# Decode attention over two KV caches: K groups and V groups put into two nested TensorE loops, and the loads put into the same order

## The chip, the cores and the metric

One core of a Trainium2 chip. The metric is the device time of one execution in microseconds (us), lower is better. The kernel before took 262.8 us in the median of its first three runs (261.95 to 264.19). "Span" below is the time from the first to the last instruction in a trace; the measured time is about 1.8 us longer than the span in the runs that were profiled. PE is TensorE, DVE is VectorE, ACT is ScalarE, SP is SyncE, which issues the loads here.

## The reference

Two independent decode attentions, A and B, with one query token, 32 query heads, 16 KV heads, head size 128 and a cache of 8192 rows. A uses only the last 2048 rows. The outputs are laid side by side.

```python
def attention(x, k_cache, v_cache, wq, wo, W):      # A: W = 2048, B: W = 8192
    q = (x @ wq).reshape(1, 1, 32, 128).transpose(0, 2, 1, 3)
    k = jnp.repeat(k_cache[:, :, 8192 - W:, :], 2, axis=1)
    v = jnp.repeat(v_cache[:, :, 8192 - W:, :], 2, axis=1)
    p = softmax(jnp.einsum("bhqd,bhkd->bhqk", q, k) * 128 ** -0.5)
    o = jnp.einsum("bhqk,bhkd->bhqd", p, v)
    return o.transpose(0, 2, 1, 3).reshape(1, 1, 4096) @ wo       # x: (1, 1, 576), all bf16
```

Every byte of K, V, wq and wo is used once: 102.8 MB are read, in both kernels.

## The kernel before

K and V are loaded in groups of four slots of 2.1 MB each: group 0 is A, groups 1 to 4 are B. There are four slot buffers for K and four for V. PE transposes K (two halves, "units", per slot), ACT and DVE evict the transposes, PE forms the scores. After K groups 0, 2 and 4 a softmax follows; its result is transposed on PE in the next odd round. PE's work stands in one loop over seven rounds; V of a group is worked on two rounds after its K (LAG = 2). What a round doesn't have is jumped over.

```python
    K_ON = lambda g: g < 5
    V_ON = lambda g: g >= LAG
    ...
    ORDER = ["k0", "k1", "k2", "v0", "v1", "k3", "v2", "v3"]
    for g in range(5 + LAG):
        for what in ORDER:                       # the order in which SP asks for the loads
            s = int(what[1])
            if what[0] == "k" and g < 5:
                load_kv(ks, g, s, kslots, "k", ...)
            if what[0] == "v" and g >= LAG:
                load_kv(vs, g - LAG, s, vslots, "v")
        ...                                      # [cut: wo loads]
        k_on, v_on = g < 5, g >= LAG
        if k_on:
            ...                                  # [cut: q_stage]
            k_transpose(g, 0, 0)
            k_transpose(g, 1, 1)
        if g % 2 == 1:
            softmax_transpose(g, 2)
            scores_zero((g, 2.5, ODD))
        if k_on:
            for u in range(2, 6):
                k_scores(g, u - 2, 2 * u)
                k_transpose(g, u, 2 * u + 1)
            k_scores(g, 4, 12)
        if v_on:
            v_slot(g - LAG, 0, 13)               # 2 x 64 matmuls between two K steps
            v_slot(g - LAG, 1, 14)
        if k_on:
            k_transpose(g, 6, 15)
            k_scores(g, 5, 16)
            k_transpose(g, 7, 17)
            k_scores(g, 6, 18)
        if v_on:
            v_slot(g - LAG, 2, 19)
        if k_on:
            k_scores(g, 7, 20)
            if g in (0, 2, 4):
                softmax_exp(CHUNK[g])
        if v_on:
            v_slot(g - LAG, 3, 21)
            v_keep(g - LAG)
```

The last argument of a step is its place in the loop body. PE's loop is written out from these places: one body, cut into blocks by condition.

```python
            with eng.Fori(0, rounds) as i:
                ...                              # [cut]
                while places:
                    cond = body[places[0]].loop[2]
                    ...                          # n: as many places as share the condition
                    with eng.If(cond(i)):
                        some(places[:n])
                    places = places[n:]
```

A load is issued by SP in program order, and waits there until its slot's last reader is done; so a load that has to wait also holds those behind it (in the trace, A's V loads, whose slots' last reader starts at 28.7 us, go out at 83.61 us, right behind a row of K loads that ends at 83.57 us).

## Time and profile before

| | kernel before |
|---|---|
| time, median (4 runs in all) | 263.5 us |
| span of the profiled run | 259.5 us |
| bytes read | 102.76 MB |
| share of the span that PE / ACT / DVE are busy | 66% / 34% / 31% |
| load rate from 10 to 55 us, and from 90 to 240 us | 427 and 429 GB/s |
| load rate from 55 to 90 us | 292 GB/s (mean of the seven windows below) |

First the page: busy shares, then 40 slices of 6.5 us with the granted clock of PE in tenths, the busy tenths of the DMA engines and the rate. The last line is the DMA queue of kind "instruction", with its packets and MB.

```profile
span 259.5 us, 7521 instructions
PE 172.1 (66%) x3406; PEld 134.3 (52%) x3406; DVE 80.9 (31%) x152; ACT 87.5 (34%) x92; POOL 12.9 (5%) x49
...
PEclk9996589957799999995998586899599555555577
DMA  7999999995478999999999999999999999999992
GB/s 280 394 450 414 434 429 414 442 419 182 200 283 330 422 427 428 437 424 429 432 422 437 424 427 432 422 437 427 424 434 419 437 427 424 434 420 433 429 400 87
...
q8 instruction: 8, 0.13, 0.2%
```

The DMA engines are at nine tenths in all slices but the first, the last and slices 9 to 12 (counted from 0): the loads bound this kernel, and the slices from about 58 to 84 us are a hole in them. The table of windows shows the hole (columns: stretch in us, its length, busy us of the five engines with counts of instructions, clock, DMA share, GB/s):

```profile
55.00:60.00 5.00, 3.90 (x35) 2.95 (x36) 1.38 (x2) 1.02 (x1) 0.24 (x1) 0.50 0.80 341
60.00:65.00 5.00, 3.46 (x45) 2.00 (x43) 3.18 (x4) 1.02 (x1) 0.24 (x1) 0.82 0.64 210
65.00:70.00 5.00, 2.61 (x36) 2.46 (x34) 1.51 (x4) 4.84 (x5) 0.00 (x0) 0.86 0.55 229
70.00:75.00 5.00, 5.00 (x71) 4.24 (x70) 3.17 (x7) 1.76 (x3) 0.00 (x0) 0.80 0.45 141
75.00:80.00 5.00, 5.00 (x86) 3.91 (x84) 2.85 (x5) 3.96 (x5) 0.24 (x1) 1.00 0.87 333
80.00:85.00 5.00, 5.00 (x85) 3.90 (x83) 2.85 (x5) 3.96 (x5) 0.24 (x1) 1.00 0.95 387
85.00:90.00 5.00, 4.25 (x68) 2.64 (x66) 2.37 (x4) 3.03 (x4) 0.47 (x2) 1.00 0.98 403
```

Against 428 GB/s these seven windows lack 4.8 MB, which is 11.1 us of loading.

SP's timeline (start, duration, what, how many; a merged row includes the waits between its issues) shows when it asked for K group 1's last slot, for three slots of K group 2, and for A's first V slots:

```profile
60.92 0.53 SPq L368 DMA_DIRECT2D kslots<-in_B_k_cache_dram  x1
...
71.60 11.97 SPq L368 DMA_DIRECT2D kslots<-in_B_k_cache_dram  x3
83.61 1.25 SPq L368 DMA_DIRECT2D vslots<-in_A_v_cache_dram  x2
```

And PE's timeline in the first round (in brackets: idle time before the row and what ended it; PEq is PE's own sequencer, and "issue" means that PE waited for nothing that the profile shows):

```profile
47.76 0.63 PE L469 MATMUL sacc<-kt,qst 128*32 128x512 bf16 x8
50.78 2.79 PE L449 MATMUL ktps<-ident,kslots 128*128 128x128 bf16 x31 [2.39 <-PEq L208]
56.10 0.29 PE L449 MATMUL ktps<-ident,kslots 128*128 128x128 bf16 x1 [2.52 <-issue]
56.32 1.04 PE L469 MATMUL sacc<-kt,qst 128*32 128x512 bf16 x8
57.29 3.59 PE L449 MATMUL ktps<-ident,kslots 128*128 128x128 bf16 x32
60.82 1.58 PE L469 MATMUL sacc<-kt,qst 128*32 128x512 bf16 x16
63.93 1.95 PE L449 MATMUL ktps<-ident,kslots 128*128 128x128 bf16 x32 [1.54 <-PEq L208]
```

K group 1's last slot goes out at 60.92 us because the last 32 transposes of group 0 are read until then (57.29 + 3.59). PE works at half clock (0.50 granted from 55 to 60 us; 3.59 us for 32 transposes that take 1.96 us elsewhere).

### The profile page before, as it was taken

What the parts mean: (1) busy time and instruction counts of PE and PEld (TensorE: products, weight loads), DVE (VectorE), ACT (ScalarE), POOL (GpSimd) and SP (SyncE); (2) the same over time, 40 slices, a digit from 0 to 9 for tenths busy, and PEclk for the clock granted to TensorE, in tenths of its full rate; (3) what the DMA queues carried; (4) which work ended last, traced back from release to release, by engine and by line L of the source; (5) the groups of instructions that cost most, each with busy time, mean ns of one, the idle gap of its engine ahead of it and who ended that gap; (6) DMA issues with size and microseconds to landing.
All of it is one profiled execution on the core that took longest, in us unless ns stands there. A gap on an engine that the chain in (4) does not pass through costs nothing. (4 is left out here: it accounts for less than half of the span.)

```text
span 259.5 us, 7521 instructions
## 1 busy us (share of the span) xinstructions
PE 172.1 (66%) x3406; PEld 134.3 (52%) x3406; DVE 80.9 (31%) x152; ACT 87.5 (34%) x92; POOL 12.9 (5%) x49
## 2 busy tenths in 40 slices
PE   0264899667699899954995684994574235335665
PEld 0131296445677687834884563883553234224565
DVE  0010245325365465333751122551144002004220
ACT  2000067423857688541671331771332000000000
POOL 7510000000000000000000000000000000000000
PEclk9996589957799999995998586899599555555577
DMA  7999999995478999999999999999999999999992
GB/s 280 394 450 414 434 429 414 442 419 182 200 283 330 422 427 428 437 424 429 432 422 437 424 427 432 422 437 427 424 434 419 437 427 424 434 420 433 429 400 87
DMA packets 8235, 102.92 MB, mean 397 GB/s; under 512 B 1184, under 2 KB 1312, under 8 KB 2080
## 3 DMA queue, kind: packets, MB, share of 16 engines
q1 hardware_dynamic: 7936, 102.77, 94.3%
q8 instruction: 8, 0.13, 0.2%
q10 hardware_dynamic: 288, 0.00, 0.1%
q14 instruction: 3, 0.02, 0.0%
HBM read 102.76 MB, written 0.00 MB: 396 GB/s over the span
## 5 line engine op out<-in xcount | busy, mean ns | idle before, releaser
L449 PE MATMUL ktps<-ident,kslots 128*128 128x128 bf16 x1280 | 89.8, 236 | 23.6 <-PEq L208 21.0
L449 PEld LDWEIGHTS ktps<-ident,kslots 128*128 128x128 bf16 x1280 | 83.2, 107 | 39.7 <-issue 39.7
L455 ACT ACTIVATE kt<-ktps 128x1024 bf16<-128x1024 bf16 x80 | 78.1, 1022 | 71.0 <-PE ktps L449 71.0
L458 DVE COPY kt<-ktps 128x1024 bf16<-128x1024 bf16 x80 | 55.3, 691 | 84.7 <-PE ktps L449 84.7
L540 PE MATMUL opsum<-vslots,ptm 128*32 128x128 bf16 x1280 | 28.4, 257 | 32.8 <-PEq L208 32.8
L540 PEld LDWEIGHTS opsum<-vslots,ptm 128*32 128x32 bf16 x1280 | 24.9, 116 | 38.5 <-issue 37.0
L469 PE MATMUL sacc<-kt,qst 128*32 128x512 bf16 x320 | 27.0, 411 | 0.9 <-issue 0.5
L403 PE MATMUL opsum<-vslots,xpad 128*32 128x512 bf16 x64 | 8.4, 508 | 16.8 <-DVE xpad L388 11.3
L549 DVE TENSOR_TENSOR diag<-opsum,rows 128x512 f32<-128x512 f32 x5 | 3.5, 691 | 43.1 <-PE opsum L540 43.1
L579 ACT ACTIVATE stat<-stat 128x1 f32<-128x1 f32 (+1 forms) x2 | 0.6, 295 | 45.9 <-DVE stat L577 45.9
L403 PEld LDWEIGHTS opsum<-vslots,xpad 128*32 128x32 bf16 x64 | 2.2, 117 | 20.0 <-issue 12.8
L435 POOL COPY qst<-qtm 128x64 bf16<-128x64 bf16 x20 | 4.6, 237 | 139.4 <-PE sacc L469 131.5
L409 ACT ACTIVATE qrow<-opsum 128x512 bf16<-128x512 f32 x2 | 1.2, 597 | 25.8 <-PE misc L403 25.8
L506 ACT ACTIVATE psb<-sacc,stat 128x2048 bf16<-128x2048 f32 x3 | 5.9, 1968 | 10.0 <-DVE stat L500 10.0
L469 PEld LDWEIGHTS sacc<-kt,qst 128*32 128x32 bf16 x320 | 5.3, 95 | 6.9 <-issue 3.0
L403 PE MATMUL misc<-vslots,xpad 128*32 128x512 bf16 x64 | 8.5, 512 | 0.0
L411 DVE CAST qrow<-misc 128x512 bf16<-128x512 f32 x2 | 1.4, 692 | 17.4 <-PE misc L403 17.4
L626 PE MATMUL ktps<-kslots,opj 128*32 128x144 bf16 x184 | 5.3, 305 | 0.8 <-DVE opj L614 0.8
L626 PEld LDWEIGHTS ktps<-kslots,opj 128*32 128x32 bf16 x184 | 4.9, 137 | 1.0 <-issue 1.0
L610 PE MATMUL misc<-acc,pick 128*128 128x32 f32 x16 | 3.0, 343 | 2.5 <-DVE acc L604 1.8
L498 DVE TENSOR_REDUCE stat<-sacc 128x1 f32<-128x1024 f32 x3 | 3.7, 1225 | 2.9 <-PE sacc L469 2.9
L610 PEld LDWEIGHTS misc<-acc,pick 128*128 128x128 f32 x16 | 2.8, 260 | 2.8 <-DVE acc L604 2.0
(66 smaller groups left out, 56.7 us busy)
## 6 DMA issues: line engine op xcount, KB each, us to landing
kslots<-in_B_k_cache_dram SPq DMA_DIRECT2D x16, 2048.0 KB, 22.3
vslots<-in_B_v_cache_dram SPq DMA_DIRECT2D x16, 2048.0 KB, 26.7
kslots<-in_A_k_cache_dram SPq DMA_DIRECT2D x4, 2048.0 KB, 30.0
vslots<-in_A_v_cache_dram SPq DMA_DIRECT2D x4, 2048.0 KB, 19.4
vslots<-in_A_wq_dram SPq DMA_DIRECT2D x2, 2048.0 KB, 9.8
vslots<-in_B_wq_dram SPq DMA_DIRECT2D x2, 2048.0 KB, 20.1
kslots<-in_A_wo_dram SPq DMA_DIRECT2D x2, 2016.0 KB, 23.6
kslots<-in_B_wo_dram SPq DMA_DIRECT2D x1, 2016.0 KB, 31.1
```

The source lines that it names most:

```text
L403: ins = pe.matmul(qps[c][32 * j:32 * j + 32, :], lhsT=xpad[:, P, x, :], rhs=src[:, o:o + 512], start=(u == 0), stop=(u == WQ_UNITS - 1))
L435: add("pool", lambda pool: pool.tensor_copy(qst[:, s * 64:(s + 1) * 64], qtm[:, o:o + 64]), reads=[("qtm", KIND[g])], writes=[("qst", s)], ...
L449: ins = pe.matmul(ktps_bf[q][:, t * 128:(t + 1) * 128], lhsT=kslots[:, s, o:o + 128], rhs=ident[:, :], start=True, stop=True, is_transpose ...
L455: add("act", lambda act, q=q, dst=dst: act.activation(dst, ktps_bf[q], ACT.Copy), reads=[("bank", q)], writes=[("kt", u % NKT, q)], tag="e ...
L458: add("dve", lambda dve, q=q, dst=dst: dve.tensor_copy(dst, ktps_bf[q]), reads=[("bank", q)], writes=[("kt", u % NKT, q)], tag="e%d%d" % ( ...
L469: ins = pe.matmul(sacc[32 * j:32 * j + 32, 512 * half:512 * half + 512], lhsT=qst[:, s * 64 + e * 32:s * 64 + e * 32 + 32], rhs=rhs, start ...
L498: add("dve", lambda dve: dve.tensor_reduce(st(P, C_M + k), sacc[:, :], AX.X, ALU.max), reads=B_S, writes=[("st", P, C_M + k)], tag="max")
L506: return act.activation(psb[:, :].rearrange("p (x g) -> p x g", g=2), src, ACT.Exp, bias=st(P, C_NB + k), scale=SCALE, accum_out=st(P, C_L ...
L540: ins = pe.matmul(opsum[32 * j:32 * j + 32, s * DH:(s + 1) * DH], lhsT=ptm[:, o:o + 32], rhs=vslots[:, s, b * 128:(b + 1) * 128], start=(u ...
L549: return dve.tensor_tensor(diag[:, g % 2, :, :], opsum[:, :].rearrange("p (s d) -> p d s", s=NS), m, ALU.mult)
L610: ins = pe.matmul(misc[:, 0:32], lhsT=pick[:, r, :], rhs=acc[:, d, 32 * r:32 * r + 32], start=(r == 0), stop=(r == 3))
L626: ins = pe.matmul(ktps[P][32 * j:32 * j + 32, 0:OUTW], lhsT=opj[:, P, jj:jj + 32], rhs=view[:, o:o + OUTW], start=(jj == 0), stop=(jj == H ...
```

## The change

The intent is to have V of A loaded while PE works on K group 1, and to have the program of PE and the order of loads agree: PE gets an outer loop over V groups, with an inner loop over the K groups that go before each (0 and 1, then V of A; 2 and 3, then V of group 1; 4, then V of group 2; and the last two V groups). So the code of all K steps now lies in one piece, with the code of the V steps behind it.

```diff
-            places = sorted(body)
-            with eng.Fori(0, rounds) as i:
-                ... [cut: one body, cut into blocks by condition]
+            inner = sorted(p for p in body if body[p].loop[2] is not None)
+            with eng.Fori(0, self.outer) as v:
+                with eng.Fori(*self.rounds_of(v)) as g:
+                    while inner:
+                        ... [cut: blocks by condition, as before]
+                some(sorted(p for p in body if body[p].loop[2] is None))
...
+    V_OF = {1: 0, 3: 1, 4: 2, 5: 3, 6: 4}          # V group worked on at the end of round g
...
-    ORDER = ["k0", "k1", "k2", "v0", "v1", "k3", "v2", "v3"]
-    for g in range(5 + LAG):
-        for what in ORDER:
-            ... [cut]
+    for g in range(7):
+        if g < 5:
+            for s in range(NS):
+                load_kv(ks, g, s, kslots, "k", ...)
+        if g in V_OF:
+            for s in range(NS):
+                load_kv(vs, V_OF[g], s, vslots, "v")
...
-            for u in range(2, 6):
+            for u in range(2, 8):
                 k_scores(g, u - 2, 2 * u)
                 k_transpose(g, u, 2 * u + 1)
-            k_scores(g, 4, 12)
-        if v_on:
-            v_slot(g - LAG, 0, 13)
-            v_slot(g - LAG, 1, 14)
-        ... [cut: the rest of the K steps, with v_slot 2 and 3 between]
+            k_scores(g, 6, 16)
+            k_scores(g, 7, 17)
+            if g in (0, 2, 4):
+                softmax_exp(CHUNK[g])
+        if g in V_OF:
+            for s in range(NS):
+                v_slot(V_OF[g], s, 20 + s, g)
+            v_keep(V_OF[g])
```

The semaphore waits are derived from the order of the program; their small adaptation is cut. Matmuls, evictions and bytes are the same.

## The prediction

> **What bounds the kernel now.** The loads. The 40-slice page has the DMA engines at 9 tenths in all slices but the first, the last and slices 9 to 12; the table of windows gives 424 to 434 GB/s from 10 to 55 and from 90 to 240 us. 102.9 MB at 428 GB/s is 240 of the 259.5 us span. PE (66%), ACT (34%) and DVE (31%) have slack overall. The chain that ended last begins at 233 us (last V slot's matmuls): a 24 us tail of small steps, beside which wo loads until 254 us.
>
> **The hole.** In 5 us windows from 55 to 90 us the rates are 341, 210, 229, 141, 333, 387, 403 GB/s: 10.2 MB where 428 GB/s would move 15.0, so 11.1 us are lost. By SP's timeline and waits, each K slot of groups 1 and 2 is issued only when PE has transposed its old content (60.9, 71.6, about 77, 83 us), and A's V loads, whose slots are free since about 29 us, stand behind group 2's third slot and go out at 83.6 us. The rate is 0 at 61 and at 69 to 72 us. PE is held up there by A's mask, maximum and exp (DVE 1.23 + 1.22, ACT 1.97 us) and by half clock. [...] 0.50 from 53 to 61 us, 32 transposes in 3.59 instead of 1.96 us.
>
> **The change.** Same bytes, matmuls and evictions. A's V loads move directly behind K group 1's last slot (out at 61 to 64 us), A's V matmuls (4 x 1.07 us) behind K group 1. Other V loads keep their rounds, but stand behind four K loads instead of between them. PE gets nested loops: a few more branches (gaps at present ones 0.4 to 1.5 us) on an engine with slack.
>
> **Estimate.** Of the 11.1 us, 3.6 are lost from 56 to 64 us, before anything changes: they stay. From 62 us one K and four V slots queue 10.5 MB, 24.5 us, to 87 us; by then K group 2's first three slots are issued, so the 7.5 us after 64 close. Later, at 2.46 us per half slot of K on PE: V of A at 89 to 94, group 2 to 114; group 3's slots are issued at about 98, 103, 108, 113 us while the queue reaches to 106 and beyond; at 113 us, when B's first V is issued, about 8 us of queue are left. After that PE waits for loads as before, and the tail is unchanged but 7.5 us earlier. Span about 252, time 262.8 - 7.7 = 255.1 us, range 252.5 to 258.5. Faster by over 2% (under 257.5): 0.86; within 2%: 0.13; slower: 0.01.
>
> **What would show it.** A's V issued at 61 to 64 us; over 400 GB/s from 64 to 90 us and on; a dip only at 57 to 64 us; last V matmuls near 225.5 us; the same 24 us tail.
>
> **What would make it wrong.** (1) A new hole at 105 to 125 us, where K groups 2 and 3 follow each other: half clock there (3.6 + 1.0 us per half slot) would eat the 8 us. (2) Loop entry and exit costing several us each. (3) K slot 3 landing late because V shares the queue. (4) A longer tail where the last matmuls meet the wo loads.

## The result, and the profile after

The changed kernel is correct and took 252.34 us in the median of four runs (251.49 to 252.97), against 263.5 us for the kernel before in its four: ratio 0.958, 95% interval 0.9516 to 0.9644. A ratio here is the mean time of one kernel's fast runs over that of the other's in the same rounds, so not quite the ratio of the medians quoted. The time lies just below the range of the prediction (252.5 to 258.5).

On another chip, in 6 runs, the changed kernel took 251.62 us against 260.89 us for the kernel before, ratio 0.9641. The changed kernel is very steady (251.15 to 252.97 over both sets); the kernel before isn't (258.16 to 264.65 over all the sets).

The page after (span 251.2 us): the busy tenths of the DMA engines and the rate in 40 slices of 6.3 us:

```profile
DMA  7999999999999999999999999999999999999980
GB/s 274 396 432 422 432 425 428 417 436 428 428 427 423 428 420 436 421 431 428 431 423 431 431 431 423 431 431 428 425 428 436 423 433 425 433 418 425 423 332 3
```

The hole is gone in full. From the third slice to the 38th none is below 417 GB/s. The first two windows of the former hole:

```profile
55.00:60.00 5.00, 1.30 (x25) 1.16 (x23) 2.63 (x5) 3.46 (x4) 0.00 (x0) 1.00 0.99 423
60.00:65.00 5.00, 5.00 (x89) 4.23 (x87) 3.40 (x7) 3.15 (x4) 0.00 (x0) 1.00 1.03 439
```

SP asks for K group 1's last slot with the third (a merged row, its second issue ends at 52.78 us), and for A's V from 52.83 us on, 8 us sooner than the prediction had it:

```profile
47.14 5.64 SPq L373 DMA_DIRECT2D kslots<-in_B_k_cache_dram  x2
52.83 2.55 SPq L373 DMA_DIRECT2D vslots<-in_A_v_cache_dram  x4
```

And PE, in the same first round, has neither gap nor half clock (1.00 granted from 45 to 55 us):

```profile
47.61 1.96 PE L459 MATMUL ktps<-ident,kslots 128*128 128x128 bf16 x32
49.50 0.82 PE L479 MATMUL sacc<-kt,qst 128*32 128x512 bf16 x8
50.26 1.96 PE L459 MATMUL ktps<-ident,kslots 128*128 128x128 bf16 x32
52.15 0.63 PE L479 MATMUL sacc<-kt,qst 128*32 128x512 bf16 x8
53.15 0.63 PE L479 MATMUL sacc<-kt,qst 128*32 128x512 bf16 x8 [0.37 <-PEq L213]
```

Group 0's scores end at 53.8 us instead of 62.4 us. This is before the moved loads could have done anything: the two kernels issue the same loads in the same order up to K group 1's last slot.

From the last V slot on, the tail has become a little longer. The chain of waits (start, duration, what), before:

```profile
233.20 2.13 PE opsum L540 x64
...
253.50 3.55 PE ktps L626 x112
```

and after:

```profile
223.25 1.92 PE opsum L550 x49
...
244.68 4.06 PE ktps L636 x96
```

The last V slot's matmuls start 9.95 us earlier, and 1.65 us of that are given back by the end of the span (from there to the end: 26.3 us before, 27.95 us after), mostly in the wo matmuls (`ktps`; the last row and one that is cut: 3.50 and 3.55 us before, 4.05 and 4.06 us after) and in small fp32 matmuls; the granted clock of this stretch was 0.62 before and 0.54 after. The rest of the measured 11.1 us is difference between runs: the run of the kernel before that was profiled took 261.28 us, less than its four timed runs (261.95 us or more), and that of the changed kernel was its slowest (252.97 us).

### The profile page after: what moved, and what is told of

It reads as the page before. It is cut to its first block, busy times and chain, and to the rows that moved or that the text cites. A ratio compares the mean times of both kernels' runs of the same rounds, so it can differ in the third digit from the quotient of the medians.

```text
span 251.2 us, 7501 instructions
## 1 busy us (share of the span) xinstructions
PE 167.9 (67%) x3406; PEld 130.6 (52%) x3406; DVE 80.6 (32%) x152; ACT 86.7 (35%) x92; POOL 12.9 (5%) x49
## 3 DMA queue, kind: packets, MB, share of 16 engines
q1 hardware_dynamic: 7936, 102.77, 96.7%
## 5 line engine op out<-in xcount | busy, mean ns | idle before, releaser
L459 PEld LDWEIGHTS ktps<-ident,kslots 128*128 128x128 bf16 x1280 | 76.3, 101 | 28.8 <-issue 28.8
L459 PE MATMUL ktps<-ident,kslots 128*128 128x128 bf16 x1280 | 82.4, 226 | 12.8 <-PEq L213 12.8
L550 PE MATMUL opsum<-vslots,ptm 128*32 128x128 bf16 x1280 | 29.9, 268 | 39.7 <-PEq L213 39.3
L550 PEld LDWEIGHTS opsum<-vslots,ptm 128*32 128x32 bf16 x1280 | 26.3, 121 | 44.2 <-issue 44.1
L479 PE MATMUL sacc<-kt,qst 128*32 128x512 bf16 x320 | 25.9, 392 | 2.0 <-PEq L213 1.8
L636 PE MATMUL ktps<-kslots,opj 128*32 128x144 bf16 x184 | 5.9, 326 | 0.7 <-DVE opj L624 0.7
L620 PE MATMUL misc<-acc,pick 128*128 128x32 f32 x16 | 3.8, 404 | 2.5 <-DVE acc L614 1.8
L620 PEld LDWEIGHTS misc<-acc,pick 128*128 128x128 f32 x16 | 3.6, 328 | 2.9 <-DVE acc L614 2.1
```

Source lines behind the costliest of these rows:

```text
L459: ins = pe.matmul(ktps_bf[q][:, t * 128:(t + 1) * 128], lhsT=kslots[:, s, o:o + 128], rhs=ident[:, :], start=True, stop=True, is_transpose ...
L479: ins = pe.matmul(sacc[32 * j:32 * j + 32, 512 * half:512 * half + 512], lhsT=qst[:, s * 64 + e * 32:s * 64 + e * 32 + 32], rhs=rhs, start ...
L550: ins = pe.matmul(opsum[32 * j:32 * j + 32, s * DH:(s + 1) * DH], lhsT=ptm[:, o:o + 32], rhs=vslots[:, s, b * 128:(b + 1) * 128], start=(u ...
L620: ins = pe.matmul(misc[:, 0:32], lhsT=pick[:, r, :], rhs=acc[:, d, 32 * r:32 * r + 32], start=(r == 0), stop=(r == 3))
L636: ins = pe.matmul(ktps[P][32 * j:32 * j + 32, 0:OUTW], lhsT=opj[:, P, jj:jj + 32], rhs=view[:, o:o + OUTW], start=(jj == 0), stop=(jj == H ...
```

## The experiments

Two theories. **FETCH**: in the kernel before, PE's first pass through the loop body jumps over V code and runs into code of its own that isn't there yet; this holds it from 48 to 56 us, leaves the array at half clock, delays K group 1's last slot from about 52.5 to 60.9 us, and so makes part of the hole. **ORDER**: the load order alone closed the hole, and what changed before 61 us is chance, or a load that landed sooner (called LANDING where it is tested alone).

Reading for FETCH: the page has a DMA queue of kind "instruction" (q8) that moves 8 packets, 0.13 MB, so about 16 KB each, and from 45 to 72 us there are four of them before and one after. That these are blocks of PE's program, and that PE waits for one after a jump, was the assumption when the theory was written; what speaks for it is in sections 3, 4 and 6. Those of the kernel before begin at 47.9, 53.7, 60.7 and 66.7 us, and PE's transposes of the first round and the next resume at 50.78, 56.10, 63.93 and 68.28 us (the last of these waits for A's softmax too, as it does in the changed kernel). These are the lines of that queue for 45 to 72 us, before, then after:

```profile
q8 instruction: 4, 0.07, 1.0%
```

```profile
q8 instruction: 1, 0.02, 0.3%
```

Over the whole execution the changed kernel's page has the same 8 packets: the change doesn't save packets, it moves them. Three of them now begin at 77.8, 84.0 and 90.2 us, where PE comes to the V code and then to the next K group. PE's pauses there (4.07 us before 86.34 us, 2.68 us before 91.09 us) end with landings, of A's last V slot at about 86.2 us and of K group 2's first slot at about 91.0 us. So PE waits for loads there anyway, and the queue of loads stays full (423 GB/s or more in each window from 75 to 95 us).

All experiments gave correct results. The kernels of one call shared a chip and the runs of the kernel before: its medians were 261.51, 260.79 and 260.89 us in the three calls.

| kernel | time, median (range), us | ratio to before, 95% interval |
|---|---|---|
| loads alone | 254.3 (251.88 to 256.97) | 0.9729 (0.965 to 0.9807) |
| two loops, old loads | 269.68 (265.54 to 270.46) | 1.0255 (1.0124 to 1.0386) |
| the same with 128 skipped matmuls | 277.0 (275.16 to 280.38) | 1.0594 (1.0522 to 1.0666) |
| one loop, V code last | 257.9 (257.37 to 259.8) | 0.991 (0.9841 to 0.9979) |
| two loops, nothing moved ahead | 256.07 (252.48 to 256.93) | 0.9794 (0.9706 to 0.9882) |
| the same, V loads of A ahead | 251.26 (250.79 to 252.97) | 0.9692 (0.9633 to 0.975) |
| before, K slot 3 asked for early | 260.91 (259.46 to 261.74) | 1.0031 (0.9972 to 1.0091) |
| change with 128 skipped matmuls | 255.86 (254.04 to 258.35) | 0.9836 (0.9776 to 0.9897) |
| whole change, again | 251.62 (251.15 to 251.88) | 0.9641 (0.9595 to 0.9688) |
| loads alone, again | 254.8 (252.75 to 257.5) | 0.9799 (0.9742 to 0.9856) |
| change with 8 skipped matmuls | 251.76 (251.33 to 253.1) | 0.9668 (0.9617 to 0.9719) |
| change with weights before the last V | 251.46 (250.94 to 251.66) | 0.964 (0.9594 to 0.9686) |

The profiled runs of three of these (both with 128 skipped matmuls, and "two loops, nothing moved ahead") were over 1.5% above the fastest of their kernel and count as slow; their traces are used for the place and kind of the waits, and the sizes of gaps and holes quoted from them are those of slow runs. Medians and ranges in the table are of all runs; the ratios are of fast runs alone, which were only three of six for "two loops, old loads" and for "two loops, nothing moved ahead".

### 1. The load order alone

```diff
-            if what[0] == "v" and g >= LAG:
+            if what[0] == "v" and g > LAG:
                 load_kv(vs, g - LAG, s, vslots, "v")
+        if g == 1:
+            for s in range(NS):
+                load_kv(vs, 0, s, vslots, "v")
```

> Kernel before, with only A's four V loads moved up behind K group 1's last slot; the PE program is untouched. FETCH theory (in the kernel before, PE's first pass through the loop body jumps over V code that is not yet used, and waits there for pages of its own program; that, not a load, holds PE from 48 to 56 us, leaves it at half clock, and sends K group 1's last slot out at 60.9 us): those gaps stay, the last slot of K group 1 still goes out near 61 us, a hole of about 3.6 us stays at 57 to 64 us, the 7.5 us after it close: ratio to before 0.966 to 0.976, about 255.5 us. ORDER theory (the load order alone closed the whole hole, the earlier start of the second K group was chance or a load that landed sooner): ratio 0.958 as for the whole change, about 252.3 us.

Measured: ratio 0.9729, 254.3 us. In the trace PE's gaps are there (2.33 us at the same row, then 3.98 us), the slot goes out at 61.27 us, and a hole stays where FETCH puts it. Its two windows, all others from 40 to 230 us being at 419 GB/s or more:

```profile
55.00:60.00 5.00, 3.55 (x32) 2.60 (x33) 1.12 (x2) 1.02 (x1) 0.24 (x1) 0.59 0.82 347
60.00:65.00 5.00, 3.46 (x37) 1.76 (x36) 2.87 (x4) 1.02 (x1) 0.24 (x1) 0.73 0.56 174
```

Against 428 GB/s that is 3.9 us. So the load order does what the prediction said of it, and no more.

The same kernel ran again beside the whole change:

> The whole change again, on the chip and in the rounds of the three runs below, since the kernel before has read 258 to 264 us on different chips and rounds: ratio 0.958 to 0.970, 251.5 to 253 us, no hole between 10 and 240 us.

> The load order alone, again, beside the whole change: FETCH theory says 2.5 to 4 us slower than the whole change (the hole at 57 to 64 us), so about 255.5 us, ratio 0.970 to 0.981. If the early start of K group 1 has no worth: equal to the whole change within 1 us.

Measured: 251.62 us for the whole change and 254.8 us for the loads alone, 3.2 us apart, as FETCH says. The single runs of the loads alone spread from 252.75 to 257.5 us, those of the whole change from 251.15 to 251.88 us. The profiled run here was the fastest, 252.75 us, and its trace shows the same two gaps (2.40 and 2.12 us) but the array at full clock after the second: the granted clock is 0.51 from 50 to 53.5 us and 1.00 from 53.5 to 63.5 us. Group 0 ends at 59.4 us instead of 63.0 us, the slot goes out at 57.88 us, and the hole is small:

```profile
55.00:60.00 5.00, 3.88 (x57) 2.28 (x57) 2.61 (x4) 1.94 (x2) 0.47 (x2) 1.00 1.01 403
60.00:65.00 5.00, 2.48 (x32) 2.25 (x32) 2.76 (x4) 2.83 (x3) 0.00 (x0) 0.87 0.97 387
```

Two traces of one kernel, so this is an observation, not a proof: how long half clock lasts after the gaps (to 53.5 us here; from 55.9 to 62.7 us in the run of 255.31 us above) may make some us of difference from run to run.

### 2. The two loops alone, with the old order of loads

```diff
-        if g < 5:
-            for s in range(NS):
-                load_kv(ks, g, s, ...)
-        if g in V_OF:
-            for s in range(NS):
-                load_kv(vs, V_OF[g], s, vslots, "v")
+        # k0 k1 k2 v0 v1 k3 v2 v3 in every round; round 2's K and A's V in this order too,
+        # asked for ahead of A's V matmuls, which stay behind K group 1
```

> The changed kernel's two loops (K code in one piece, V code behind it), with the old order of loads (three slots of K group 2 ahead of A's V). FETCH theory: no gap at 48 to 56 us, K group 0's last scores end near 53.8 us, K group 1's last slot goes out near 52.3 us while the queue reaches to about 66 us, the next slots follow at about 62, 68, 73 us: no hole or one under 1 us, ratio 0.956 to 0.966, about 252.5 us, although the load order is the old one. ORDER theory: the hole stays, at most its first 3.6 us are gained, ratio 0.985 to 1.0.

Measured: ratio 1.0255, far from both expectations. The first half of the expectation held: PE has no gap in round 0, group 0's scores end at 54.4 us, the slot goes out at about 52.8 us, and the old hole shrinks to 2.9 us (351, 393, 323 and 400 GB/s from 60 to 80 us). But a mistake of the experiment's design opened a new hole: A's V is worked on before K group 2 and loaded behind it. PE waits for V until 110.4 us, with K group 2 lying in its slots, and nothing can be loaded (smaller dips, to 161 GB/s at 115 us and 259 GB/s at 190 us, follow later):

```profile
105.00:110.00 5.00, 2.04 (x80) 1.80 (x75) 0.00 (x0) 0.00 (x0) 0.00 (x0) 0.50 0.23 95
110.00:115.00 5.00, 4.71 (x62) 4.47 (x51) 2.76 (x4) 2.16 (x3) 0.00 (x0) 0.55 0.00 0
```

What follows: PE's order may not run ahead of the load order. With V moved one round earlier on PE alone, the kernel is slower than before. (The other way round it works: in sections 1 and 7 the loads alone are moved ahead, with a gain.)

### 3. The same, with code that is never executed

A block of 128 matmuls under a condition that is never true, jumped over before the seventh unit's transposes, at the place where the kernel before jumps over two V slots (also 128 matmuls).

```diff
                     while inner:
+                        if inner[0] == 13:
+                            with eng.If(((g + g) & 1) == 1):
+                                ... [128 matmuls of zeros, PE only]
                         cond = body[inner[0]].loop[2]
```

> As the run before this one (two loops, old load order), with 128 matmuls that are never executed put between the sixth and seventh K transposes of the loop body and jumped over, as the kernel before jumps over V code there. FETCH theory: PE stands still again for 2 to 5 us at that place in K group 0 only, with pages of program arriving there, falls to half clock, K group 1's last slot goes out at 57 to 61 us, and a hole of 5 to 11 us returns: ratio 0.975 to 1.0. If the two loops themselves or anything else but the skipped code made the difference: same as the run before, 0.956 to 0.966.

Measured: 277.0 us against 269.68 us without the block in the same rounds, 7.3 us more by these medians, and 276.5 against 268.0 us, 8.6 us more, in the mean of the fast runs alone (the ratio of the expectation was upset by run 2's mistake, the difference wasn't). PE's gaps are back in round 0 alone:

```profile
48.05 0.63 PE L490 MATMUL sacc<-kt,qst 128*32 128x512 bf16 x8
51.02 3.46 PE L470 MATMUL ktps<-ident,kslots 128*128 128x128 bf16 x31 [2.34 <-PEq L214]
56.78 0.22 PE L470 MATMUL ktps<-ident,kslots 128*128 128x128 bf16 x1 [2.29 <-issue]
```

Nothing but code that doesn't run was added, and it brings back both gaps at the same two rows: after the first jump, and before the 32nd transpose. The "instruction" queue now moves 9 packets in all instead of 8 (and 10 in the last kernel of this list, where another 256 matmuls of PE are written out; so these are taken to be blocks of PE's program, one for about 128 matmuls, an estimate from these two counts): the program is about one block longer, and one packet more is moved. Whether a block that is jumped over as a whole would be fetched isn't shown: the skipped code has about the length of one block by that estimate, but nothing shows that it begins at a block's start. In the next round the same jump shows no gap: in the kernel before, the transposes behind it start at 83.50 us, while the scores ahead of it still run (82.93 us, 0.63 us long). By the same estimate the loop of the kernel before, with about 600 matmuls, is nearly five blocks long; it runs seven rounds, and the whole execution moves 8 packets, none of them between 68 and 200 us.

### 4. The changed kernel with 128, and with 8, skipped matmuls

The same block in the changed kernel, and a control with the same branches but a short jump.

> The changed kernel, with 128 never executed matmuls jumped over between the sixth and seventh K transposes. FETCH theory: PE's gaps at 48 to 57 us come back in K group 0 alone, K group 1's last slot goes out at about 60.5 us, a hole of 3 to 4 us at 57 to 64 us: ratio to before 0.966 to 0.976, like the run with the load order alone. Otherwise 0.958.

> Control for the never executed code: the same pair of branches at the same place in the changed kernel, but only 8 matmuls are jumped over instead of 128. If the distance jumped is what costs (FETCH), no gap above 1 us at that place and the time of the whole change within 1 us; if the branches cost, a gap of some us, as with 128.

Measured: 255.86 us with 128 (0.9836), 251.76 us with 8 (0.9668); the whole change had 251.62 us, on the chip of the second. With 128 PE shows gaps of 2.60 and 3.66 us at the two rows, and the slot goes out at 61.36 us. With 8, the rows read:

```profile
49.03 0.63 PE L490 MATMUL sacc<-kt,qst 128*32 128x512 bf16 x8
49.59 2.27 PE L470 MATMUL ktps<-ident,kslots 128*128 128x128 bf16 x32
```

So it isn't the branch that costs, but the length of what it jumps over. Nor is it the length of the program as such: the last kernel of this list has 256 matmuls more, behind the loop, and PE's idle time before all its K transposes is 13.8 us, against 12.7 us in the whole change and 17.6 us with the 128. The ratio of 0.9836 is above the expected 0.966 to 0.976; the runs of the kernel before were lower here (median 260.79 us) than in the first set (263.5 us), and two further dips to 338 and 357 GB/s stood in that trace, a slow run. The kernel of section 7 that loads without a hole took 251.26 us on the chip where the 128 took 255.86 us, and the 8 matched the whole change on theirs: these two comparisons carry the point.

### 5. Was it a load that PE waited for?

```diff
-                 (2, 1, kslots[:, 3, P * WQ_U:(P + 1) * WQ_U], ("k", 3, P))]
+                 (2, 1, wq3[:, P, :], ("wq3", P))]      # its own buffer: A's K slot 3 is free at once
```

> Kernel before, with the last third of each wq in a buffer of its own, so that A's fourth K slot is asked for at about 5 us instead of 30 us and lands some 2 us sooner. LANDING rival (PE stood from 48.4 to 56.1 us for that slot): the gap shrinks or goes, ratio 0.96 to 0.985. FETCH theory: the gap of about 2.4 and 2.5 to 4 us stays at the same two places, ratio 0.99 to 1.01.

Measured: 1.0031, no gain. The slot's load was asked for at about 6 us and landed after 40.6 us, at about 46.5 us; in the kernel before it was asked for at 30.2 us and landed after 16.4 us, at 46.6 us. So it did not land sooner, as was expected of this run, for it stands in the same queue (q1, which moves all 102.77 MB of loads); but PE came to the place 1.7 us sooner, and its gaps moved along (1.94 us before a row that now starts at 48.63 instead of 50.78 us, then 2.83 us). With the same landing, PE resumed 2.1 us after it in one kernel and 4.2 us after it in the other. The wait isn't for that load. As the slot didn't land sooner, this run alone wouldn't decide; but in the kernel before, too, it had landed 1.8 us before PE stopped.

### 6. One loop, with only the V code put last

```diff
-        if v_on:
-            v_slot(g - LAG, 0, 13)
-            v_slot(g - LAG, 1, 14)
...
-            v_slot(g - LAG, 3, 21)
+            for s in range(NS):
+                v_slot(g - LAG, s, 21 + s)
```

> Kernel before: one loop, lag of two rounds and its order of loads kept, only the V matmuls moved from between the K steps to the end of the loop body, so that the K code lies in one piece. FETCH theory: like the two loops with the old load order, no gap at 48 to 56 us, no hole, ratio 0.956 to 0.968. If it took the two loops or V of A one round earlier: the hole stays, ratio 0.985 to 1.0.

Measured: 0.991, a miss, in the range that was written for the rival. The gaps in the middle of round 0 are gone and its scores end at 52.8 us, but the jump over all of V now stands at the end of the body, and the gap with it, again followed by half clock (0.5 in the slice from 57.6 to 64.0 us):

```profile
52.14 0.63 PE L469 MATMUL sacc<-kt,qst 128*32 128x512 bf16 x8 [0.37 <-PEq L208]
59.10 5.61 PE L449 MATMUL ktps<-ident,kslots 128*128 128x128 bf16 x64 [6.33 <-PEq L208]
```

In the changed kernel the next 64 transposes start at 54.0 us; part of the 6.33 us is the wait for A's softmax, which the changed kernel has too (3.70 us). Two packets of the queue of kind "instruction" begin between 55 and 62 us, and it moves 10 in all instead of 8, though no code was added; which blocks the two more are isn't known. Of the old hole 4.1 us stay (344, 301, 313 and 400 GB/s from 60 to 80 us). Besides, the old load order made a new hole at 185 to 190 us (180 GB/s), where V loads wait for V work that now comes later in the round. So the second loop isn't a matter of taste: it is what lets PE go back to the next K group without passing over V code.

### 7. Two loops with nothing moved ahead, and then the loads alone ahead

V of A back behind K group 2, on PE and in the loads; then its loads alone ahead.

```diff
-    V_OF = {1: 0, 3: 1, 4: 2, 5: 3, 6: 4}
+    V_OF = {2: 0, 3: 1, 4: 2, 5: 3, 6: 4}
...
-        if g in V_OF:
-            for s in range(NS):
-                load_kv(vs, V_OF[g], s, vslots, "v")
+        vg = {1: 0, 3: 1, 4: 2, 5: 3, 6: 4}.get(g)      # second kernel only
+        if vg is not None:
+            for s in range(NS):
+                load_kv(vs, vg, s, vslots, "v")
```

> The changed kernel with A's V loads and A's V matmuls both put back behind K group 2 (three K groups in the first inner loop, loads K0 K1 K2 V0 K3 V1 K4 V2 V3 V4). So the code of the K steps lies in one piece and no V code is skipped in the first rounds, but nothing is moved ahead. FETCH theory: no gap at 48 to 56 us, K group 0's scores end near 54 us, K group 1's last slot out near 52.5 us; a smaller hole stays at 60 to 80 us, 3 to 5 us instead of 11.1, because K slots alone wait for PE there: ratio 0.968 to 0.982. If the gap was not the cause: as before, 0.99 to 1.0.

> As the run before this one, with A's V loads alone moved ahead of K group 2's; A's V matmuls stay behind K group 2. Both parts of the gain are then there and only the early V matmuls are missing: ratio 0.954 to 0.964, as the whole change. If the early matmuls matter (V slots come free sooner), 0.966 or more, with a new hole when the V loads of the next group wait for A's V matmuls.

Measured: 0.9794 for the first, inside its expected range: PE has no gap at 48 to 56 us, and a hole of 4.4 us stays (344, 380, 257, 406 and 380 GB/s from 60 to 85 us, in a slow run). For the second, 0.9692 with 251.26 us. That ratio is above the 0.954 to 0.964 that was written for it and in the range of its rival (0.966 or more); but the new hole that the rival foretold isn't there (no window of 5 us from 55 to 240 us is below 414 GB/s), and its time is that of the whole change on two other chips (251.62 and 252.34 us). The kernel before ran lower on this chip (260.79 us) than in the first set (263.5 us). The loads of the second kernel run without a hole, at 416 GB/s or more in all windows from 55 to 85 us. What follows: the loop layout alone is worth about 2%, the load order alone 2 to 2.7%, together 3 to 4%. That V's matmuls stand one round earlier shows no gain of its own, as far as times of different chips can be compared; the two kernels didn't run in the same rounds.

### 8. A try at the tail

The last V group's matmuls were taken out of the loop, and the softmax weights of A and B put ahead of them.

> The changed kernel with the last V group's matmuls behind the loop and the softmax weights of A and B (7.5 us of small steps in the tail's chain) ahead of them: the chain from the last V slot to the end falls from 27 to about 20 us, the end is then set by the wo loads (DMA busy until about 243.6 us): 247 to 249 us, ratio 0.940 to 0.955.

Measured: 251.46 us, a miss: the same as the change (251.62 us in the same rounds). The weights no longer stand in the chain after the last V slot, but the loads of wo end no sooner, and the chain that ended last now goes through a load (start, duration, what):

```profile
218.02 28.07 DMA vslots<-in_B_wo_dram
```

It landed at 246.09 us, and 0.9 us of matmuls and a copy follow before the output is written. No version here beats the changed kernel by more than noise.

## Why the prediction was right or wrong

- **Right: what bounds the kernel, and where the hole is.** Loads at 424 to 434 GB/s and one hole of 11.1 us; the changed kernel gained 11.1 us in its first set (9.3 us on another chip, by the medians). That the first figure equals the hole is luck: between the two profiled runs the span fell by 8.3 us, 9.95 us up to the last V slot less 1.65 us in the tail.
- **Right: what the load order does.** It was priced at 7.5 us, leaving 3.6 us. With the load order alone, 7.2 and 6.1 us were gained (by the medians), and the trace shows 3.9 us of hole left at 55 to 65 us in one run.
- **Wrong: "Of the 11.1 us, 3.6 are lost from 56 to 64 us, before anything changes: they stay."** They went, because something does change before that. The step that failed is "PE gets nested loops: a few more branches (gaps at present ones 0.4 to 1.5 us) on an engine with slack". The loops were costed by their branches alone, and what they do to the first pass through the code was missed. The rows with 2.39 and 2.52 us of idle time in round 0 were in the trace before; the prediction put PE's delay down to the softmax of A and to half clock, and the half clock (0.50 from 51.5 to 61.8 us) came after the first gap; in the changed kernel (two traces) and in the one with 8 skipped matmuls, which don't have the two gaps, the clock is 1.00 from 50 to 55 us. Without the jump the slot goes out at about 52.3 us instead of 60.92 us, the queue never empties, and the change gains 3.2 us over the load order alone in the same rounds.
- **Wrong with it: the signs.** A's V went out at 52.8 us, not 61 to 64 us; no dip stayed at 57 to 64 us. The last V slot's matmuls started at 223.25 us instead of 225.5 us.
- **Right: no new hole at 105 to 125 us.** K groups 2 and 3, back to back, kept their lead (429 to 433 GB/s).
- **Slightly wrong: the tail.** It was to be the same; it grew by 1.65 us in the profiled pair, at the lower clock (0.54 against 0.62).
- **"An engine with slack" was true on average and false where it mattered.** PE is busy 66% of the span, but in round 0 it decides when the next K slots may be asked for.

What stays open: why PE resumes only 1.6 to 3.2 us after such a packet has begun (which takes about 1.1 us), and why the second gap stands before the 32nd transpose, isn't shown by any record; and that the wait is for a block of the program is concluded from the coincidence with the packets and from the runs with skipped code, not read from a semaphore.

## What to carry to other kernels

Read the gaps of an engine's first pass through a loop apart from those of later passes: a long jump over code that isn't used yet can stop the engine there. In the traces here a jump over 128 matmuls came with two gaps, of 1.9 to 2.6 us and of 2.1 to 4.0 us (2.39 and 2.52 us in the kernel before, where the way from the start of the same scores, at 47.76 us and in the changed kernel at 47.04 us, to the end of K group 0, half clock included, took 14.64 us against 6.74 us); a jump over 8 matmuls showed no gap, and neither did the jump in the next round. Lay out code so that the first rounds run straight on: what is skipped at first belongs behind, with an inner loop that doesn't pass over it. And an engine with slack still sets the pace where its progress frees the buffers of the next loads; whatever it is to work on first must also be loaded first.
